# Moving the exp of 3 of 16 key tiles from ScalarE to VectorE in a fused attention and MLP block

## The chip, the cores and the metric

The kernel runs on one core of one Trainium2 chip. The metric is the device time of one execution in microseconds (us). PE is the matmul engine (TensorE) and PEld its weight loads, ACT is ScalarE, DVE is VectorE, POOL is GpSimd. SBUF and PSUM are the memories on the chip that these kernels use; the matmuls write to PSUM. A few executions of each kernel were timed. Executions over 1.5% slower than the fastest of the same kernel are left out of the means. Ratios are the mean time of one kernel's fast runs over the mean of the other's fast runs of the same rounds, on the same chip, so they are not quite the ratios of the medians that are quoted beside them. The rounds ran on several chips; the kernel before stayed within 1122 to 1131 us in all of them, so a difference of two medians from different rounds is good to a few us and no better.

## The reference, cut to what matters

```python
def _A_ref(x, wqkv, wo):                       # B=1, S=2048, D=512, 32 heads of 16
    qkv = (x @ wqkv)...                        # q, k, v: [heads, S, 16]
    scores = jnp.einsum('bhqd,bhkd->bhqk', q, k) * Dh ** (-0.5)
    p = softmax(scores)                        # 32 x 2048 x 2048 exps
    o = jnp.einsum('bhqk,bhkd->bhqd', p, v)
    return o... @ wo
h = layernorm(x) * (1 + ca) + sa               # modulation from silu(c) @ w_mod
x = x + ga * _A_ref(h, A_wqkv, A_wo)
h = layernorm(x) * (1 + cb) + sb
x = x + gb * MLP(h)                            # 512 -> 1376 -> 512, gelu
```

There are 134 million exps against a head dimension of only 16, so the exp is a large share of the work.

## The kernel before

Work goes in 32 *runs*: 4 query blocks of 512, times 8 groups of 4 heads. Each run walks 16 key tiles of 128. For one key tile PE makes the scores of 4 heads as two *QK pairs* (two 32-row matmuls side by side, 128 keys x 512 queries each), ScalarE takes the exp of each pair (one 128x1024 activation), and PE multiplies by V with one *PV unit*: four column-tiled matmuls, one for each head. V has a column of ones, so the softmax denominator comes out of the same matmuls. PE's order is written by hand; the other engines are scheduled by the framework.

```python
stp = tile_pool(name="stp", bufs=3, space=psum)   # score buffers, 128x1024 f32 each
odp = tile_pool(name="odp", bufs=1, space=psum)   # od: PV sum of a run, 128x512 f32
axp = tile_pool(name="axp", bufs=1, space=psum)   # projections and MLP, 128x512 f32
ptp = tile_pool(name="ptp", bufs=3)               # exp tiles (here 4 heads each)
...
def emit_exp(s):
    pt = ptp.tile([P, 4, QB], BF16, name="pt")
    for half in range(2):
        nc.scalar.activation(out=pt[:, 2 * half:2 * half + 2, :], in_=st_of.pop(2 * s + half),
                             func=ACT.Exp, scale=ESC)
...
def emit_pv(s):
    for i in range(4):
        nc.tensor.matmul(out=od[32 * i:32 * i + 32, :], lhsT=VE[kt][:, 8 * cc + 2 * i + par, :],
                         rhs=pt[:, i, :], start=(kt == 0), stop=(kt == NT - 1),
                         tile_position=(0, 32 * i))
...
for s in range(NS):                # one key tile of one run
    emit_exp(s)
    emit_qk(2 * s + 3); emit_qk(2 * s + 4)
    emit_pv(s - 1)
    pop()                          # one piece of a projection, of Wo or of the MLP, if any waits
```

The softmax here doesn't subtract the row's maximum and nothing guards it: scores larger than these inputs give would overflow.

## Time and profile before

| | before |
|---|---|
| time | 1125.75 us (median of 3, 1123.66 to 1128.4) |
| exps on ScalarE | 1024, 0.92 us of busy time each |
| ScalarE idle before exps | 26 us |
| PE clock granted, mean | 0.66 |

The page of the kernel before: the busy line, and the rows of PE, ACT and the granted PE clock over 40 equal slices, each digit in tenths.

```profile
PE 950.4 (85%) x4984; PEld 234.6 (21%) x4984; DVE 193.9 (17%) x364; ACT 985.4 (88%) x1057; POOL 62.9 (6%) x75
...
PE   0678899989999869999999789989898698999856
...
ACT  0367999999999999999999999999999999999801
...
PEclk9988955555557967555558977555558976555568
```

Next the exps as one group of its instructions (busy us, mean ns of one, then the idle time before them and what ended it), and the two waits between PE and the exps (us in total, times, longest).

```profile
L255 ACT ACTIVATE pt<-st 128x1024 bf16<-128x1024 f32 x1024 | 942.1, 1261 | 25.7 <-PE st L248 25.5
```

```profile
PE st L248 <- ACT pt L255: 50.6, 79, 7.8
ACT pt L255 <- PE st L248: 25.5, 28, 1.4
```

ScalarE sets the pace: it is full in every slice between start and tail, and it waits for scores only 28 times. PE is second, and only just: it shows 85% busy. A stretch of its timeline at half clock shows how the time of one key tile (1.83 us, PV at 503.90 to PV at 505.73) is spent.

```profile
503.08 3.89 ACT L255 ACTIVATE pt<-st 128x1024 bf16<-128x1024 f32 x4
503.36 0.61 PE L248 MATMUL st<-qm_3970,kT_0_173 32*128 32x512 bf16 x2
...
503.90 0.62 PE L267 MATMUL od<-pt,VE_190 128*32 128x512 bf16 x4
...
504.45 1.35 PE L248 MATMUL st<-qm_3970,kT_0_173 32*128 32x512 bf16 x4
...
505.73 0.62 PE L267 MATMUL od<-pt,VE_191 128*32 128x512 bf16 x4
```

A QK pair to the next PV takes 0.54 us, a PV to the next pair 0.55 us. So PE needs, by this estimate, about 2 x 0.54 + 0.55 = 1.63 us of the 1.83 us.

### The profile page before, as it was taken

How to read it: one execution, taken by the hardware profiler on the slowest of the kernel's cores; microseconds unless marked ns; L12 is line 12 of the kernel's file. 1: busy time of each engine (PE TensorE's matmuls, PEld its weight loads, DVE VectorE, ACT ScalarE, POOL GpSimd, SP SyncE). 2: the span in 40 equal slices, each digit the busy share in tenths (PEclk: the TensorE clock that was granted, in tenths of full speed). 3: DMA queues.
4: the chain of work that ended last, by engine and by line, in shares of the span. 5: the costliest groups of instructions: out<-in, count | busy, mean ns of one | idle time of the engine just before them, and what ended most of it. 6: DMA issues, size and time to landing. Idle time of an engine off the chain costs nothing.

```text
span 1122.1 us, 12537 instructions
## 1 busy us (share of the span) xinstructions
PE 950.4 (85%) x4984; PEld 234.6 (21%) x4984; DVE 193.9 (17%) x364; ACT 985.4 (88%) x1057; POOL 62.9 (6%) x75
## 2 busy tenths in 40 slices
PE   0678899989999869999999789989898698999856
PEld 0222311111112312111112222111112222111122
DVE  3412200000004411000004311000005211000053
ACT  0367999999999999999999999999999999999801
POOL 5000000000000000000000000000000000000000
PEclk9988955555557967555558977555558976555568
DMA  9300000000000000000000000000000000000000
GB/s 259 104 0 1 11 11 11 11 11 11 11 11 11 11 5 25 11 11 11 11 11 11 12 10 21 11 11 10 11 11 11 11 25 11 6 11 11 11 10 19
DMA packets 27772, 22.25 MB, mean 20 GB/s; under 512 B 13921, under 2 KB 22466, under 8 KB 27714
## 3 DMA queue, kind: packets, MB, share of 16 engines
q1 hardware_dynamic: 24546, 18.83, 5.8%
q10 hardware_dynamic: 3168, 2.62, 0.9%
q8 instruction: 39, 0.64, 0.2%
q14 instruction: 19, 0.16, 0.0%
HBM read 18.81 MB, written 2.62 MB: 19 GB/s over the span
## 4 chain that ended last, share of the span: by engine, by line
ACT 63%; PE 17%; issue 13%; DMA 4%; DVE 2%; SPq 0%; POOL 0%; POOLq 0%; ACTq 0%; DVEq 0%
ACT pt L255 61%; PE st L248 3%; PE ax L199 3%; PE ax L355 3%; PE od L267 2%; PE st L222 2%; DMA xb<-in_A_x_dram 2%; PE st L355 1%; PE st L336 1%; DMA hT<-in_w_mod_dram 1%; DMA W_116<-in_B_w_dram 1%; PE st L404 0%; PE ax L300 0%; ACT big L345 0%; ACT hT L184 0%
## 5 line engine op out<-in xcount | busy, mean ns | idle before, releaser
L255 ACT ACTIVATE pt<-st 128x1024 bf16<-128x1024 f32 x1024 | 942.1, 1261 | 25.7 <-PE st L248 25.5
L276 DVE COPY OD<-od 128x512 f32<-128x512 f32 x32 | 22.2, 692 | 424.2 <-PE od L267 380.3
L289 POOL TENSOR_TENSOR OT<-OD,RB 128x512 bf16<-128x512 f32 x32 | 40.5, 1267 | 912.8 <-DMA RB<-rn 912.8
L345 ACT ACTIVATE big<-big 128x5632 bf16<-128x5632 bf16 x4 | 19.6, 4896 | 37.6 <-DVE big L338 37.6
L355 PE MATMUL ax<-W_116,big 128*128 128x512 bf16 x132 | 39.1, 420 | 0.0
L336 PE MATMUL ax<-big,W_113 128*128 128x512 bf16 x132 | 33.8, 378 | 3.4 <-DVE big L338 2.2
L338 DVE TENSOR_SCALAR big<-ax,b1c 128x512 bf16<-128x512 f32 x33 | 24.8, 751 | 36.7 <-PE ax L336 36.7
L184 ACT ACTIVATE hT<-st,modA 128x512 bf16<-128x512 bf16 x8 | 6.2, 777 | 28.0 <-DVE hT L187 28.0
L199 PE MATMUL ax<-hT,Wq_93 128*128 128x512 bf16 x60 | 24.8, 560 | 0.1
L156 PE MATMUL ax<-sc,hT 128*128 128x1 bf16 x32 | 1.0, 165 | 27.3 <-DVE sc L137 27.3
L222 PE MATMUL st<-Wq_95,hT 128*128 128x512 bf16 x64 | 19.1, 439 | 5.4 <-ACT VE_183 L226 0.7
L359 DVE TENSOR_TENSOR res<-ax,gb_bc 128x512 f32<-128x512 f32 x12 | 8.3, 692 | 87.4 <-PE ax L355 87.4
L336 PEld LDWEIGHTS <-W_113 128*128 128x128 bf16 x176 | 17.0, 99 | 24.5 <-issue 11.7
L281 DVE RECIPROCAL dc<-dc 128x16 f32<-128x16 f32 x32 | 8.0, 251 | 80.7 <-DMA dc<-dn 80.7
L355 PEld LDWEIGHTS <-big 128*128 128x128 bf16 x176 | 15.1, 104 | 30.6 <-issue 15.9
L309 DVE TENSOR_TENSOR res<-ax,ga_bc 128x512 f32<-128x512 f32 x12 | 8.3, 692 | 68.0 <-PE ax L306 68.0
L267 PE MATMUL od<-pt,VE_187 128*32 128x512 bf16 x128 | 18.7, 574 | 0.0
L267 PE MATMUL od<-pt,VE_192 128*32 128x512 bf16 x128 | 18.2, 539 | 0.4 <-ACT pt L255 0.3
L267 PE MATMUL od<-pt,VE_188 128*32 128x512 bf16 x128 | 18.5, 567 | 0.0
L248 PEld LDWEIGHTS <-kT_2_167 32*128 32x128 bf16 x128 | 7.7, 94 | 51.5 <-issue 51.0
L267 PE MATMUL od<-pt,VE_183 128*32 128x512 bf16 x128 | 18.0, 553 | 0.0
L267 PE MATMUL od<-pt,VE_182 128*32 128x512 bf16 x128 | 18.0, 553 | 0.0
(336 smaller groups left out, 1202.3 us busy)
## 6 DMA issues: line engine op xcount, KB each, us to landing
RB<-rn SPq DMA_DIRECT2D x128, 64.0 KB
big<-in_w_mod_dram SPq DMA_DIRECT2D x1, 2048.0 KB
out_dram<-o SPq DMA_DIRECT2D x16, 128.0 KB
xb<-in_A_x_dram ACTq DMA_DIRECT2D x3, 512.0 KB
W_113<-in_B_w_dram SPq DMA_DIRECT2D x1, 1376.0 KB
W_116<-in_B_w_dram SPq DMA_DIRECT2D x1, 1280.0 KB
hT<-in_w_mod_dram ACTq DMA_DIRECT2D x2, 512.0 KB
xb<-in_A_x_dram SPq DMA_DIRECT2D x1, 512.0 KB
```

The source lines that it names most:

```text
L199: nc.tensor.matmul(out=ps, lhsT=w[:, j, cc * P:(cc + 1) * P], rhs=hT[b][:, j, :], start=(j == 0), stop=(j == NC - 1))
L222: nc.tensor.matmul(out=ps, lhsT=hT[b][:, j, tt * P:(tt + 1) * P], rhs=Wq[2][:, j, :], start=(j == 0), stop=(j == NC - 1))
L248: nc.tensor.matmul(out=st[:, g, :], lhsT=kT[cc][kb][rows, ko * P:(ko + 1) * P], rhs=qm[(cc, b, par)][rows, :], start=True, stop=True)
L255: nc.scalar.activation(out=pt[:, 2 * half:2 * half + 2, :], in_=st_of.pop(2 * s + half), func=ACT.Exp, scale=ESC)
L267: nc.tensor.matmul(out=od[32 * i:32 * i + 32, :], lhsT=VE[kt][:, 8 * cc + 2 * i + par, :], rhs=pt[:, i, :], start=(kt == 0), stop=(kt == N ...
L276: nc.vector.tensor_copy(out=OD, in_=od)
L289: nc.gpsimd.tensor_tensor(out=ot, in0=OD, in1=RB, op=ALU.mult)
L309: nc.vector.tensor_tensor(out=y, in0=ps, in1=ga_bc, op=ALU.mult)
L336: nc.tensor.matmul(out=ps, lhsT=W1[:, j, f * P:(f + 1) * P], rhs=state["h"][:, j, :], start=(j == 0), stop=(j == NC - 1))
L338: nc.vector.tensor_scalar(out=state["g"][:, f, :], in0=ps, scalar1=b1c[:, f:f + 1], scalar2=None, op0=ALU.add)
L345: nc.scalar.activation(out=g, in_=g, func=ACT.Gelu_apprx_tanh)
L355: nc.tensor.matmul(out=ps, lhsT=state["g"][:, f, t * P:(t + 1) * P], rhs=W2[:, f, :], start=False, stop=(f == NF - 1))
```

## The change

The intent: VectorE is idle 83% of the time, so let it make some exps. Adding a bias to the scaled score and converting to int16 gives bits that, read as bf16, are a piecewise linear 2^x. To reduce the error (for one reading it lies between -3.9% and +2.0%, for six between -0.12% and +0.07%, worked out from the formula), the integer is shifted by five further amounts, the six bf16 *readings* go through PV with V scaled by six weights, and the sum is the mean. Key tiles 2, 7 and 11 of every run are treated so; the other 13 stay on ScalarE. The diff, cut to its core:

```diff
+    NPH = 6
+    PH_SH = [round(128 * j / NPH) for j in range(NPH)]
+    PH_W = [bf16_round(2.0 ** (-sh / 128)) for sh in PH_SH]
+    DK = [2, 7, 11]
-    stp = tile_pool(name="stp", bufs=3, space=psum)
+    stp = tile_pool(name="stp", bufs=2, space=psum)
+    sdp = tile_pool(name="sdp", bufs=1, space=psum)    # scores for VectorE, 128x1024 f32
-    ptp = tile_pool(name="ptp", bufs=3)                # tiles of 4 heads
+    ptp = tile_pool(name="ptp", bufs=5)                # tiles of 2 heads
+    dpp = tile_pool(name="dpp", bufs=3)                # the readings ph0 to ph5
 ...
+    def emit_dexp(n, r, kt, half):
+        sd = sdp.tile([P, 1024], FP32, name="sd")
+        qk(sd..., r, kt, half)
+        ph0 = dpp.tile([P, 1024], I16, name="ph0")
+        nc.vector.tensor_scalar(out=ph0, in0=sd, scalar1=PH_B, scalar2=0.0,
+                                op0=ALU.add, op1=ALU.max)
+        for j in range(1, NPH):
+            ph = dpp.tile([P, 1024], I16, name=f"ph{j}")
+            nc.vector.tensor_scalar(out=ph, in0=ph0, scalar1=PH_SH[j], scalar2=None, op0=ALU.add)
+        ...                                            # second half: six PV units into pvq
+            for j in range(NPH):
+                pvq.append((r, n + 4, lambda j=j, srcs=srcs: pv(r, kt, j, srcs)))
+    def emit_pv(n, budget):                            # takes ready units, oldest due first
+        ...
+            q = min(ready, key=lambda q: (q[0], q[1]))
 ...
+        for n in range(len(apairs)):                   # one ScalarE exp (2 heads)
+            emit_exp(n)                                # second half: one PV unit into pvq, due n + 1
+            emit_qk(n + 2)
+            for d in dpairs.get(n, ()):
+                emit_dexp(n, *d)
+            emit_pv(n, 3 if len(pvq) > 7 else 2)
+            if r > 0 and n % 3 == 0 or ...: pop()
```

(Cut: the 15 further copies of V, scaled on POOL; loads and tiles rearranged to make room.)

More of the change, by code (lines that the diff above doesn't have):

```diff
@@ L16 @@
 I32 = mybir.dt.int32
+I16 = mybir.dt.int16
 @with_exitstack
@@ L49, with bf16_round, ph_gain @@
     ESC = math.log(2.0) / 128.0
+    NPH = 6
+    PH_SH = [round(128 * j / NPH) for j in range(NPH)]
+    def bf16_round(v):
+        m, e = math.frexp(v)
+        return math.ldexp(round(m * 256) / 256, e)
+    PH_W = [bf16_round(2.0 ** (-sh / 128)) for sh in PH_SH]
+    def ph_gain():
+        tot = 0.0
+        for f in range(128):
+            val = 0.0
+            for sh, w in zip(PH_SH, PH_W):
+                n, m = divmod(f + sh, 128)
+                val += w * 2.0 ** n * (1 + m / 128)
+            tot += val / 2.0 ** (f / 128)
+        return tot / 128
+    PH_B = 127.0 * 128.0 - 128.0 * math.log2(ph_gain())
+    DK = [2, 7, 11]
     psum = bass.MemoryType.PSUM
@@ L53 @@
     keep = ctx.enter_context(tc.tile_pool(name="keep", bufs=1))
-    stp = ctx.enter_context(tc.tile_pool(name="stp", bufs=3, space=psum))
+    stp = ctx.enter_context(tc.tile_pool(name="stp", bufs=2, space=psum))
+    sdp = ctx.enter_context(tc.tile_pool(name="sdp", bufs=1, space=psum))
     odp = ctx.enter_context(tc.tile_pool(name="odp", bufs=1, space=psum))
@@ L59 @@
     work = ctx.enter_context(tc.tile_pool(name="work", bufs=2))
-    ptp = ctx.enter_context(tc.tile_pool(name="ptp", bufs=3))
+    wqp = ctx.enter_context(tc.tile_pool(name="wqp", bufs=3))
+    ptp = ctx.enter_context(tc.tile_pool(name="ptp", bufs=5))
+    dpp = ctx.enter_context(tc.tile_pool(name="dpp", bufs=3))
     x_src = A_x[0].rearrange("(b t p) d -> b p t d", t=TPB, p=P)
@@ L65, with gbuf @@
     nc.scalar.dma_start(out=c_bf, in_=c.rearrange("o (j p) -> p (o j)", p=P))
-    xb = [xin.tile([P, TPB, D], BF16, name="xb", bufs=NQ) for _ in range(NQ)]
+    xb = [xin.tile([P, TPB, D], BF16, name="xb", bufs=2) for _ in range(NQ)]
     nc.sync.dma_start(out=xb[0], in_=x_src[0])
     wm_src = w_mod.rearrange("(j p) n -> p j n", p=P)
-    def big():
-        return work.tile([P, NC * 4 * D], BF16, name="big", bufs=1)
+    def gbuf():
+        return work.tile([P, NF, QB], BF16, name="g", bufs=1)
     def block_tile():
@@ L75 @@
     WmA = [block_tile() for _ in range(2)]
-    WmB = big().rearrange("p (j n) -> p j n", j=NC)
+    wmb = gbuf()
+    WmB = {4: wmb[:, 0:4, :], 3: wmb[:, 4:8, :],
+           2: work.tile([P, NC, D], BF16, name="x2", bufs=1)}
     for i in range(2):
@@ L79 @@
     wq_src = A_wqkv.rearrange("(j p) n -> p j n", p=P)
-    Wq = [keep.tile([P, NC, D], BF16, name=f"Wq{i}") for i in range(3)]
-    for i in (1, 0, 2):
+    Wq = {}
+    for i in (1, 2, 0):
+        Wq[i] = wqp.tile([P, NC, D], BF16, name="Wq")
         nc.sync.dma_start(out=Wq[i], in_=wq_src[:, :, i * D:(i + 1) * D])
@@ L84 @@
         nc.scalar.dma_start(out=xb[b], in_=x_src[b])
-    nc.sync.dma_start(out=WmB, in_=wm_src[:, :, 2 * D:6 * D])
+    for i in (2, 3, 4):
+        nc.sync.dma_start(out=WmB[i], in_=wm_src[:, :, i * D:(i + 1) * D])
     Wo = keep.tile([P, 8, D], BF16, name="Wo")
@@ L96, with load_w2 @@
     nc.sync.dma_start(out=W1[:, :, 0:F], in_=B_w1.rearrange("(j p) n -> p j n", p=P))
-    W2 = keep.tile([P, NF, D], BF16, name="W2")
-    nc.gpsimd.memset(W2[:, NF - 1, :], 0.0)
-    nc.sync.dma_start(out=W2[:, 0:NF - 1, :],
-                      in_=B_w2[0:(NF - 1) * P, :].rearrange("(j p) n -> p j n", p=P))
-    nc.sync.dma_start(out=W2[0:FL, NF - 1, :], in_=B_w2[(NF - 1) * P:F, :])
+    W2 = {}
+    def load_w2():
+        for i in range(3):
+            W2[i] = wqp.tile([P, NC, D], BF16, name="Wq") if i < 2 else keep.tile([P, 3, D], BF16, name="W2c")
+        for i in range(2):
+            nc.sync.dma_start(out=W2[i], in_=B_w2[4 * i * P:4 * (i + 1) * P, :].rearrange("(j p) n -> p j n", p=P))
+        nc.gpsimd.memset(W2[2][:, 2, :], 0.0)
+        nc.sync.dma_start(out=W2[2][:, 0:2, :], in_=B_w2[8 * P:10 * P, :].rearrange("(j p) n -> p j n", p=P))
+        nc.sync.dma_start(out=W2[2][0:FL, 2, :], in_=B_w2[10 * P:F, :])
     b1_bf = const.tile([P, NF], BF16, name="b1_bf")
@@ L175, in ln_rows @@
         nc.gpsimd.tensor_tensor(out=rs, in0=rs, in1=eps_c, op=ALU.pow)
-        z = work.tile([P, TPB, D], BF16, name="ln_z")
+        z = work.tile([P, TPB, D], BF16, name="ln_z", bufs=1)
         for t in range(TPB):
@@ L191 @@
     kT = [[keep.tile([P, QB], BF16, name=f"kT{cc}_{b}") for b in range(NQ)] for cc in range(NC)]
-    VE = [keep.tile([P, 32, 32], BF16, name=f"VE{t}") for t in range(NT)]
+    VW = 17
+    VE = {}
     for t in range(NT):
-        nc.gpsimd.memset(VE[t][:, :, 16:32], 1.0)
+        for ph in (range(NPH) if t in DK else (0,)):
+            v = keep.tile([P, 32 * VW + 15], BF16, name=f"VE{t}_{ph}")
+            nc.gpsimd.memset(v[:, 32 * VW:32 * VW + 15], 0.0)
+            vv = v[:, 0:32 * VW].rearrange("p (h w) -> p h w", w=VW)
+            nc.gpsimd.memset(vv[:, :, 16:17], PH_W[ph] if t in DK else 1.0)
+            VE[(t, ph)] = (v, vv[:, :, 0:16])
     OT = {}
@@ L224, in emit_v @@
         src = ps.rearrange("p (h d) -> p h d", d=16)
-        if eng is nc.scalar:
-            nc.scalar.copy(out=VE[t][:, :, 0:16], in_=src)
-        else:
-            nc.vector.tensor_copy(out=VE[t][:, :, 0:16], in_=src)
-    slots = [(b, u, kt) for b in range(NQ) for u in range(8) for kt in range(NT)]
-    NS = len(slots)
+        if t in DK:
+            vf = work.tile([P, D], FP32, name="vf", bufs=1)
+            nc.vector.tensor_copy(out=vf, in_=ps)
+            vs = vf.rearrange("p (h d) -> p h d", d=16)
+            for ph in range(NPH):
+                nc.gpsimd.tensor_scalar(out=VE[(t, ph)][1], in0=vs, scalar1=PH_W[ph],
+                                        scalar2=0.0, op0=ALU.mult, op1=ALU.add)
+        elif eng is nc.scalar:
+            nc.scalar.copy(out=VE[(t, 0)][1], in_=src)
+        else:
+            nc.vector.tensor_copy(out=VE[(t, 0)][1], in_=src)
+    NA = NT - len(DK)
+    runs = [(b, u) for b in range(NQ) for u in range(8)]
+    apairs = []
+    dpairs = {}
+    for r, (b, u) in enumerate(runs):
+        base = len(apairs)
+        for kt in range(NT):
+            if kt not in DK:
+                apairs += [(r, kt, 0), (r, kt, 1)]
+        for m, kt in enumerate(DK):
+            for half in range(2):
+                at = base + int((2 * m + half + 0.25) * 2 * NA / (2 * len(DK) + 0.5))
+                dpairs.setdefault(at, []).append((r, kt, half))
     st_of = {}
@@ L235, with qk @@
     od_of = {}
-    def emit_qk(n):
-        s, half = divmod(n, 2)
-        if s >= NS:
-            return
-        b, u, kt = slots[s]
+    left = {r: len(DK) * NPH + NA for r in range(len(runs))}
+    begun = set()
+    pvq = []
+    def qk(st, r, kt, half):
+        b, u = runs[r]
         cc, par = divmod(u, 2)
         kb, ko = divmod(kt, TPB)
-        st = st_tile().rearrange("p (g q) -> p g q", g=2)
         for g in range(2):
@@ L249, in emit_qk @@
                              rhs=qm[(cc, b, par)][rows, :], start=True, stop=True)
-        st_of[n] = st
-    def emit_exp(s):
-        pt = ptp.tile([P, 4, QB], BF16, name="pt")
-        for half in range(2):
-            nc.scalar.activation(out=pt[:, 2 * half:2 * half + 2, :], in_=st_of.pop(2 * s + half),
-                                 func=ACT.Exp, scale=ESC)
-        pt_of[s] = pt
-    def emit_pv(s):
-        b, u, kt = slots[s]
-        cc, par = divmod(u, 2)
-        if kt == 0:
-            od_of[(b, u)] = odp.tile([P, QB], FP32, name="od")
-        od = od_of[(b, u)]
-        pt = pt_of.pop(s)
+    def emit_qk(n):
+        if n < len(apairs):
+            st_of[n] = st_tile().rearrange("p (g q) -> p g q", g=2)
+            qk(st_of[n], *apairs[n])
@@ new lines, in emit_exp @@
+    def emit_exp(n):
+        r, kt, half = apairs[n]
+        if half == 0:
+            pt_of[(r, kt)] = []
+        pts = pt_of[(r, kt)]
+        pt = ptp.tile([P, 2, QB], BF16, name="pt")
+        pts.append(pt)
+        nc.scalar.activation(out=pt, in_=st_of.pop(n), func=ACT.Exp, scale=ESC)
+        if half == 1:
+            pvq.append((r, n + 1, lambda: pv(r, kt, 0, [pts[i // 2][:, i % 2, :] for i in range(4)])))
+            del pt_of[(r, kt)]
+    def emit_dexp(n, r, kt, half):
+        sd = sdp.tile([P, 1024], FP32, name="sd")
+        qk(sd.rearrange("p (g q) -> p g q", g=2), r, kt, half)
+        ph0 = dpp.tile([P, 1024], I16, name="ph0")
+        nc.vector.tensor_scalar(out=ph0, in0=sd, scalar1=PH_B, scalar2=0.0,
+                                op0=ALU.add, op1=ALU.max)
+        phs = [ph0]
+        for j in range(1, NPH):
+            ph = dpp.tile([P, 1024], I16, name=f"ph{j}")
+            nc.vector.tensor_scalar(out=ph, in0=ph0, scalar1=PH_SH[j], scalar2=None, op0=ALU.add)
+            phs.append(ph)
+        if half == 0:
+            pt_of[(r, kt)] = phs
+        else:
+            first = pt_of.pop((r, kt))
+            for j in range(NPH):
+                srcs = [t.bitcast(BF16)[:, g * QB:(g + 1) * QB]
+                        for t in (first[j], phs[j]) for g in range(2)]
+                pvq.append((r, n + 4, lambda j=j, srcs=srcs: pv(r, kt, j, srcs)))
@@ L266, in emit_pv, with pv @@
+    def pv(r, kt, ph, srcs):
+        b, u = runs[r]
+        cc, par = divmod(u, 2)
+        if r not in od_of:
+            od_of[r] = odp.tile([P, QB], FP32, name="od")
+        od = od_of[r]
+        start = r not in begun
+        begun.add(r)
+        left[r] -= 1
         for i in range(4):
-            nc.tensor.matmul(out=od[32 * i:32 * i + 32, :], lhsT=VE[kt][:, 8 * cc + 2 * i + par, :],
-                             rhs=pt[:, i, :], start=(kt == 0), stop=(kt == NT - 1),
+            c0 = VW * (8 * cc + 2 * i + par)
+            nc.tensor.matmul(out=od[32 * i:32 * i + 32, :], lhsT=VE[(kt, ph)][0][:, c0:c0 + 32],
+                             rhs=srcs[i], start=start, stop=(left[r] == 0),
@@ L269, in emit_pv @@
                              tile_position=(0, 32 * i))
-        if kt == NT - 1:
-            emit_norm(b, u)
-    def emit_norm(b, u):
-        od = od_of.pop((b, u))
+        if left[r] == 0:
+            emit_norm(r)
+    def emit_pv(n, budget):
+        while pvq and budget > 0:
+            ready = [q for q in pvq if q[1] <= n]
+            if not ready:
+                return
+            q = min(ready, key=lambda q: (q[0], q[1]))
+            if any(p[0] < q[0] for p in pvq):
+                return
+            pvq.remove(q)
+            q[2]()
+            budget -= 1
@@ L275, in emit_norm @@
+    def emit_norm(r):
+        b, u = runs[r]
+        od = od_of.pop(r)
         OD = work.tile([P, QB], FP32, name="OD")
@@ L283, in emit_norm @@
         nc.sync.dma_start(out=rn.rearrange("i (s e) -> (i s) e", e=16), in_=dc)
-        RB = work.tile([P, QB], FP32, name="RB")
+        RB = work.tile([P, QB], FP32, name="RB", bufs=1)
         for i in range(4):
@@ L287, in emit_norm @@
                               in_=rn[i:i + 1, :].to_broadcast([32, QB]))
-        ot = OT[(b, u)] = work.tile([P, QB], BF16, name="OT", bufs=11)
+        ot = OT[(b, u)] = work.tile([P, QB], BF16, name="OT", bufs=9)
         nc.gpsimd.tensor_tensor(out=ot, in0=OD, in1=RB, op=ALU.mult)
     def tail_units(b, alloc, wide):
-        x2 = work.tile([P, TPB, D], BF16, name="x2")
+        x2 = work.tile([P, TPB, D], BF16, name="x2", bufs=1)
         units = []
@@ L307, in wo_b @@
                                  start=False, stop=(u == 7))
-            y = work.tile([P, D], FP32, name="res")
+            y = work.tile([P, D], FP32, name="res", bufs=1)
             nc.vector.tensor_tensor(out=y, in0=ps, in1=ga_bc, op=ALU.mult)
-            nc.vector.tensor_tensor(out=x2[:, t, :], in0=y, in1=xb[b][:, t, :], op=ALU.add)
+            xr = work.tile([P, D], BF16, name="xr")
+            nc.sync.dma_start(out=xr, in_=x_src[b][:, t, :])
+            nc.vector.tensor_tensor(out=x2[:, t, :], in0=y, in1=xr, op=ALU.add)
         for t in range(TPB):
@@ L317, in ln @@
             state["z"] = ln_rows(lambda t: x2[:, t, :], "b")
-            buf = big()
-            state["h"] = buf[:, 0:NC * QB].rearrange("p (j q) -> p j q", j=NC)
-            state["g"] = buf[:, NC * QB:(NC + NF) * QB].rearrange("p (f q) -> p f q", f=NF)
+            state["h"] = block_tile()
+            state["g"] = gbuf()
         units.append((ln, False))
@@ L354, in w2 @@
             for f in range(lo, hi):
-                nc.tensor.matmul(out=ps, lhsT=state["g"][:, f, t * P:(t + 1) * P], rhs=W2[:, f, :],
+                nc.tensor.matmul(out=ps, lhsT=state["g"][:, f, t * P:(t + 1) * P], rhs=W2[f // 4][:, f % 4, :],
                                  start=False, stop=(f == NF - 1))
             if hi == NF:
-                y = work.tile([P, D], FP32, name="res")
+                y = work.tile([P, D], FP32, name="res", bufs=1)
                 nc.vector.tensor_tensor(out=y, in0=ps, in1=gb_bc, op=ALU.mult)
@@ L387, in mods_late, with gate @@
     def mods_late():
-        mod_columns(modB, ((WmB, 1), (WmB, 2)), aux())
+        mod_columns(modB, ((WmB[3], 0), (WmB[4], 0)), aux())
         nc.vector.tensor_scalar(out=modB[:, NC:2 * NC], in0=modB[:, NC:2 * NC], scalar1=1.0,
                                 scalar2=None, op0=ALU.add)
-    def gate(dst, w, h):
+    def gate(dst, i):
+        if i not in WmB:
+            WmB[i] = work.tile([P, NC, D], BF16, name="x2", bufs=1)
+            nc.sync.dma_start(out=WmB[i], in_=wm_src[:, :, i * D:(i + 1) * D])
+            return
+        w, h = WmB[i], 0
         ps = aux()
@@ L429 @@
                 queue.append((f"k{cc}", lambda cc=cc, b=b: emit_k(aux(), cc, b, nc.vector), False))
-        queue.append(("gate", lambda: gate(ga_bc, WmB, 0), False))
+        queue.append(("gate", lambda: gate(ga_bc, 2), False))
         queue.append(("gate", mods_late, False))
-        queue.append(("gate", lambda: gate(gb_bc, WmB, 3), False))
-        for n in range(3):
+        queue.append(("gate", lambda: gate(gb_bc, 5), False))
+        queue.append(("gate", load_w2, False))
+        queue.append(("gate", lambda: gate(gb_bc, 5), False))
+        for n in range(2):
             emit_qk(n)
-        for s in range(NS):
-            b, u, kt = slots[s]
-            cc, par = divmod(u, 2)
-            emit_exp(s)
-            if b == 0 and u == 0 and kt % TPB == 1 and kt < 12:
+        for n in range(len(apairs)):
+            r, kt, half = apairs[n]
+            b, u = runs[r]
+            at = n % (2 * NA)
+            emit_exp(n)
+            if r == 0 and half == 0 and kt % TPB == 0 and kt < 12:
                 nb = kt // TPB + 1
@@ L443 @@
                     zs[nb + 1] = ln_rows(lambda t: xb[nb + 1][:, t, :], "a")
-            if s + 2 < NS:
-                nb2, nu2, _ = slots[s + 2]
-                need(f"k{nu2 // 2}")
-                need(f"q{nu2 // 2}_{nb2}")
-            emit_qk(2 * s + 3)
-            emit_qk(2 * s + 4)
-            if s > 0:
-                emit_pv(s - 1)
-            if b == 0 and u == 0:
-                if kt >= 12:
-                    pop()
-            else:
+            if n + 4 < len(apairs):
+                b2, u2 = runs[apairs[n + 4][0]]
+                need(f"k{u2 // 2}")
+                need(f"q{u2 // 2}_{b2}")
+            emit_qk(n + 2)
+            for d in dpairs.get(n, ()):
+                emit_dexp(n, *d)
+            emit_pv(n, 3 if len(pvq) > 7 else 2)
+            if r > 0 and n % 3 == 0 or r == 0 and at > 2 * NA - 6:
                 pop()
-            if u == 0 and kt == 10 and b > 0:
+            if b > 0 and u == 0 and at == 18:
                 for fn, cont in tail_units(b - 1, aux, False):
                     queue.append(("tail", fn, cont))
-            if u % 2 == 1 and kt == 6:
+            if u % 2 == 1 and at == 4:
                 nc2, nb2 = (u // 2 + 1, b) if u < 7 else (0, b + 1)
@@ L463 @@
                     push_front(f"q{nc2}_{nb2}", lambda cc=nc2, b=nb2: emit_q(aux(), cc, b))
-        emit_pv(NS - 1)
+        while pvq:
+            emit_pv(1 << 30, 1)
         while queue:
```

## The prediction

> **What bounds the kernel now.** ScalarE. In the page's busy line ACT is at 985 us of 1122 (88%), PE 950 (85%), VectorE 194 (17%). The largest group is the exp of the scores: 1024 activations of 128x1024, 942 us, 0.92 us each; they have only 26 us of idle before them, and they hold 61% of the chain of waits. They begin 48 us into the span (timeline) and end about 64 us before its end (slices). PE looks busy, but in pure attention stretches (250 to 290, 500 to 530 us) its granted clock is 0.50 and it keeps up even so.
>
> **What the change moves.**
> - ScalarE: 832 exps instead of 1024. 192 x 0.92 = 177 us leave it.
> - VectorE: 192 units, each one 128x1024 reading of PSUM and five 16-bit additions in SBUF. From the trace, a VectorE instruction costs about 0.16 us plus 0.53 us per 512 f32 elements of PSUM (copy 692 ns), about 0.06 us more per pointer scalar[...].[...] Estimate: 1.23 + 5 x 0.43 = 3.35 us a unit, 643 us in all, VectorE about 840 us busy. In a tail stretch (Wo, MLP) it then needs 1.14 times ScalarE's time per run of 16 key tiles; elsewhere about 0.91.
> - PE: PV units (four column-tiled matmuls) per run go from 16 to 31; 4096 matmuls of attention become 6016 (QK unchanged). At full clock, with 0.11 us for each switch between QK and PV shapes (a PV unit to the next QK takes 0.32 us warm, 0.55 cold), a run needs about 18 us plus 4 us of projections and MLP; at clock 0.5 about 31 us plus 8. ScalarE needs 23.9 us.
> - PSUM: score buffers for ScalarE fall from 3 to 2, so a projection burst (4 full matmuls, near 0.95 us) between two QK pairs shows as a ScalarE stall, about 0.4 us for each of some 175.
>
> **How much is on the path.** All 177 us are, but three engines end up within some 15% of each other and wait for one another in order. Sum: 48 start + 765 exps + 70 projection stalls + 40 VectorE-bound tails + 50 block inputs and gelus + 25 low-clock stretches + 64 tail = 1062; I take 1055.
>
> **The clock decides much.** [...]the records here hold only 0.5 and 1.0. In this trace, windows of attention alone fall back to 0.5 and rise when 128x128 matmuls come in.[...]
>
> **Time:** 1055 us, range 970 to 1150; faster by over 2%: 0.70; within 2%: 0.17; slower: 0.13.
>
> **What would show it right:** 832 exps at 0.92 us, ACT busy near 808 us with 100 to 150 us more idle before exps, mostly behind PE; the 16-bit additions near 0.43 us, the PSUM reading near 1.23 us; VectorE over 75% busy; mean granted clock up from 0.66 to about 0.85; PV matmuls 3968.
>
> **What would make it wrong:** the 16-bit additions at half that rate (VectorE 1050 us or more, then slower than before); the clock staying at 0.5 in attention (PE-bound, about 1150 us); waits of PE for the single projection buffer or the single VectorE score buffer; or, the other way, stalls hidden well, near 980.

Two of its figures stand as estimates: the mean clock of 0.85, and the 0.43 us for an addition. The second can be estimated from the trace of the kernel before. There a copy of 512 f32 elements out of PSUM took 692 ns, the same with a pointer scalar 751 ns, an aggregate over 6 elements 168 ns; the 0.16, 0.53 and 0.06 us agree with these. ln_z (512 bf16 elements, two pointer scalars) took 407 ns: less 0.16 and 2 x 0.06 us, that leaves 0.13 us, so 1024 elements without a pointer would take about 0.16 + 0.26 = 0.42 us.

The times for PE are estimates as well, and the traces come near them. At full clock the trace of the changed kernel has 0.23 us from one PV unit to the next and 0.32 us from a PV unit to a QK pair (medians), so about 0.1 us more where the shape changes; at half clock 0.40 us, and 0.15 us more. 63 units a run at 0.22 us with 35 changes of shape come to about 17 us at full clock, at 0.40 us to about 30 us. The 128x512 matmuls of projections and MLP start 0.216 us apart at full clock and 0.43 us at half clock (medians in the kernel before, which has 680 of them: 4.6 and 9 us a run). A QK pair follows the last of a burst after 0.31 us at full clock: 3 x 0.216 + 0.31 = 0.96 us. The stall of 0.4 us for each burst is a mere estimate; dk0, with two score buffers, has 85 waits of exps for scores, 82 us in all. As to the clock, in the exp loop of the kernel before 177 of 193 periods of its records without a 128x128 matmul were at 0.5, and 67 of 103 with one at 1.0.

## The result, and the profile after

| | before | after |
|---|---|---|
| time (median) | 1127.08 us | 1277.05 us (1271.78 to 1289.86) |
| ratio | | 1.135 (95%: 1.125 to 1.145) |
| exps on ScalarE, idle before them | 1024, 26 us | 832, 325 us |
| VectorE busy | 194 us | 761 us |
| PE clock granted, mean | 0.66 | 0.75 |

The change made the kernel 13.5% slower. The page of the changed kernel: the busy line and the same rows.

```profile
PE 990.6 (78%) x6843; PEld 248.0 (20%) x6904; DVE 761.4 (60%) x1517; ACT 839.6 (66%) x864; POOL 74.4 (6%) x139
...
PE   2668888888888876887787886887888886878856
...
ACT  1456766777777768877766677667777767777711
...
PEclk9888766656659688887768687687659778697578
```

The busy line has 6843 records of 6904 matmuls. No engine is full any longer: between start and tail ScalarE is at 6 to 8 tenths in every slice, PE at 6 to 8. That is the picture of engines that wait for each other in turn. The exps' group and the largest waits among PE, ScalarE and VectorE in the loop:

```profile
L328 ACT ACTIVATE pt<-st 128x1024 bf16<-128x1024 f32 x832 | 796.9, 1027 | 325.2 <-PE od L364 184.2 <-PE st L313 128.5 <-PE sd L313 10.0
```

```profile
ACT pt L328 <- PE od L364: 184.2, 95, 3.7
PE st L313 <- ACT pt L328: 129.8, 201, 7.6
ACT pt L328 <- PE st L313: 128.5, 141, 4.5
PE od L364 <- DVE OD L386: 64.6, 31, 2.9
```

The first wait did not exist before. An exp does not *read* od; it waits for a PV matmul because that matmul reads the exp tile (pt) it wants to write into. With five tiles in turn (each holds 2 heads, so two and a half key tiles), the exp stands still until an older tile has been through PV. The timeline shows why that takes long (cut to matmuls and exps):

```profile
299.20 0.60 PE L313 MATMUL st<-qm_2648,kT_2_183 32*128 32x512 bf16 x2
...
299.74 0.61 PE L364 MATMUL od<-ph_2937,VE_4_203 128*32 128x512 bf16 x2
299.74 0.61 PE L364 MATMUL od<-ph_3009,VE_4_203 128*32 128x512 bf16 x2
...
300.13 0.64 PE L364 MATMUL od<-ph_2939,VE_5_206 128*32 128x512 bf16 x2
300.14 0.64 PE L364 MATMUL od<-ph_3011,VE_5_206 128*32 128x512 bf16 x2
...
301.25 0.62 PE L364 MATMUL od<-pt,VE_0_215 128*32 128x512 bf16 x4
...
301.65 0.44 PE L364 MATMUL od<-pt,VE_0_218 128*32 128x512 bf16 x4
301.96 1.94 ACT L328 ACTIVATE pt<-st 128x1024 bf16<-128x1024 f32 x2 [2.54 <-PE od L364]
...
303.04 0.39 PE L313 MATMUL st<-qm_2648,kT_2_183 32*128 32x512 bf16 x2 [0.95 <-ACT pt L328]
```

The PV units of VectorE's readings (inputs named ph) are due first and go first; the PV units of the exp tiles (input named pt) come after them. ScalarE has been idle for 2.54 us when the first of these (301.25) has been through and a tile is free. Then PE is idle for 0.95 us, because it has no score buffer until that exp is done.

VectorE itself did what was forecast. One unit, from the timeline:

```profile
303.68 1.23 DVE L337 TENSOR_SCALAR ph_3111<-sd 128x1024 int16<-128x1024 f32 x1 [3.79 <-PE sd L313]
304.94 0.43 DVE L342 TENSOR_SCALAR ph_3113<-ph_3111 128x1024 int16<-128x1024 int16 x1
305.28 0.42 DVE L342 TENSOR_SCALAR ph_3115<-ph_3111 128x1024 int16<-128x1024 int16 x1
```

The reading of the scores in PSUM takes 1.23 us and an addition 0.42 us (the medians of 192 and of 960 are the same; 13 additions took 0.6 to 1.5 us). The additions start 0.34 us apart, so a unit costs about 1.23 + 5 x 0.34 = 2.9 us, a little under the forecast 3.35 us. VectorE waited 3.79 us for its scores here: it does not set the pace at this place.

### The profile page after: what moved, and what is told of

The parts are those of the page before. It is cut to its first block, busy times and chain, and to the rows that moved or that the text cites. A ratio compares the mean times of both kernels' runs of the same rounds, so it can differ in the third digit from the quotient of the medians.

```text
span 1270.0 us, 17728 instructions
## 1 busy us (share of the span) xinstructions
PE 990.6 (78%) x6843; PEld 248.0 (20%) x6904; DVE 761.4 (60%) x1517; ACT 839.6 (66%) x864; POOL 74.4 (6%) x139
## 4 chain that ended last, share of the span: by engine, by line
PE 54%; ACT 20%; DVE 14%; issue 9%; DMA 2%; POOL 0%; ACTq 0%; SPq 0%; POOLq 0%; DVEq 0%
PE od L364 22%; PE st L313 18%; ACT pt L328 17%; PE ax L466 2%; PE ax L447 2%; PE ax L247 2%; DVE OD L386 2%; ACT g L456 2%; PE st L270 1%; DMA xb<-in_A_x_dram 1%; PE ax L416 1%; PE st L466 1%; PE ax L410 1%; PE st L447 1%; PE sd L313 1%
## 5 line engine op out<-in xcount | busy, mean ns | idle before, releaser
L328 ACT ACTIVATE pt<-st 128x1024 bf16<-128x1024 f32 x832 | 796.9, 1027 | 325.2 <-PE od L364 184.2
L456 ACT ACTIVATE g<-g 128x5632 bf16<-128x5632 bf16 x4 | 19.6, 4896 | 37.1 <-DVE g L449 37.0
L447 PE MATMUL ax<-hT,W_125 128*128 128x512 bf16 x116 | 39.7, 453 | 3.3 <-issue 1.3
L449 DVE TENSOR_SCALAR g<-ax,b1c 128x512 bf16<-128x512 f32 x33 | 24.6, 746 | 26.6 <-PE ax L447 26.6
L247 PE MATMUL ax<-hT,Wq 128*128 128x512 bf16 x99 | 33.5, 462 | 3.5 <-issue 2.0
L466 PE MATMUL ax<-Wq,g 128*128 128x512 bf16 x85 | 26.4, 427 | 1.8 <-issue 1.6
L270 PE MATMUL st<-Wq,hT 128*128 128x512 bf16 x62 | 18.7, 431 | 7.7 <-DVE vf L275 1.2
L466 PEld LDWEIGHTS <-g 128*128 128x128 bf16 x176 | 15.1, 105 | 33.8 <-issue 19.1
L247 PEld LDWEIGHTS <-Wq 128*128 128x128 bf16 x128 | 11.9, 110 | 34.7 <-issue 27.7
L212 DVE BATCH_NORM_STATS2 ln_s<-xb 128x6 f32<-128x512 bf16 x16 | 10.3, 681 | 13.2 <-DMA xb<-in_A_x_dram 13.2
```

The source lines that it names most:

```text
L247: nc.tensor.matmul(out=ps, lhsT=w[:, j, cc * P:(cc + 1) * P], rhs=hT[b][:, j, :], start=(j == 0), stop=(j == NC - 1))
L270: nc.tensor.matmul(out=ps, lhsT=hT[b][:, j, tt * P:(tt + 1) * P], rhs=Wq[2][:, j, :], start=(j == 0), stop=(j == NC - 1))
L328: nc.scalar.activation(out=pt, in_=st_of.pop(n), func=ACT.Exp, scale=ESC)
L447: nc.tensor.matmul(out=ps, lhsT=W1[:, j, f * P:(f + 1) * P], rhs=state["h"][:, j, :], start=(j == 0), stop=(j == NC - 1))
L449: nc.vector.tensor_scalar(out=state["g"][:, f, :], in0=ps, scalar1=b1c[:, f:f + 1], scalar2=None, op0=ALU.add)
L456: nc.scalar.activation(out=g, in_=g, func=ACT.Gelu_apprx_tanh)
```

## The experiments

Three theories were to be told apart. **PE theory:** the 15 extra PV units of each run (31 instead of 16) are on the path. **Buffer theory:** ScalarE starves because buffers were cut (score buffers from 3 to 2) or are held too long (five exp tiles behind the PV order). **VectorE theory:** VectorE's queue is late with the od copy and with its score buffer. All 14 kernels gave results within the tolerance of the comparison with the reference. "Before" is the kernel before in the same rounds, with medians of 1124 to 1129 us.

### 1. dk0: the rearranged code without any VectorE exp

```diff
-    DK = [2, 7, 11]
+    DK = []
```

> The restructured code with no key tile on VectorE (all 1024 exps on ScalarE, two score buffers instead of three, half-size exp tiles). If the restructuring is harmless: 1125 us, within 2% of the kernel before. If the third score buffer mattered (each projection burst then stalls ScalarE by about 0.4 us): 1170 to 1200 us, ScalarE idle before exps up from 26 to 100 us.

Measured: 1214.23 us, ratio 1.078 (1.075 to 1.082). The waits of ScalarE on PE:

```profile
ACT pt L328 <- PE st L313: 82.3, 85, 2.3
```

The rearrangement alone loses about 90 us, with all exps still on ScalarE: the second reading of the expectation, though 14 us above its range. The exps wait 82 us for scores instead of 26, and none of them waits for od, so exp tiles are not scarce here. Start to start, exps are 921 ns apart at the median instead of 905 (read off the trace); over 1024 exps that would be another 16 us.

### 2. pv1_add5: VectorE's work kept, its extra PV units dropped

```diff
+    NPV = 1
-    left = {r: len(DK) * NPH + NA for r in range(len(runs))}
+    left = {r: len(DK) * NPV + NA for r in range(len(runs))}
-            for j in range(NPH):
+            for j in range(NPV):        # PV units for the first reading only
```

(The bias is matched to one reading, so the result is a valid, coarser one.)

> VectorE does all it did (reading and five additions, the additions unused), but only one of the six readings goes into PV: PV units per run fall from 31 to 16. If PE's extra PV work (its time and its place in PE's order) is the cause: 1050 us or less, ScalarE idle before exps under 170 us. If VectorE's load is the cause (late od copy, late score buffer): it stays above 1200 us.

Measured: 1053.38 us (3 us above the range of the first reading), ratio 0.937 (0.934 to 0.939). VectorE is as busy as in the changed kernel (764 us), yet the kernel is faster than before. The VectorE theory is out as the main cause; what hurts comes in with the extra PV units.

### 3. pv6_add0: the additions dropped, the extra PV units kept

```diff
-        for j in range(1, NPH):
-            ph = dpp.tile(...); nc.vector.tensor_scalar(out=ph, in0=ph0, ...)
-                        for t in (first[j], phs[j]) for g in range(2)]
+                        for t in (first[0], phs[0]) for g in range(2)]
```

(The bias is matched to the one reading here too.)

> VectorE makes one reading only (no additions, about 1.2 us a unit instead of 3.0), but PV still has 31 units a run, all six on the same reading. PE theory: 1200 to 1280 us, little gained but the wait of PV for the od copy (65 us of PE idle in the changed kernel) shrinks to under 30. VectorE theory: 1100 us or less.

Measured: 1242.36 us, ratio 1.104 (1.101 to 1.107). The additions are worth only 35 us. PE's wait for the od copy falls from 65 to 28 us, about as much as those 35:

```profile
PE od L360 <- DVE OD L382: 28.1, 31, 1.7
```

### 4. pt_first: another order of the same PV units

```diff
-            q = min(ready, key=lambda q: (q[0], q[1]))
+            q = min(ready, key=lambda q: (q[0], q[3], q[1]))   # q[3]: 0 for ScalarE's, 1 for VectorE's
```

> Only the order of PV units on PE changes: a ready unit of ScalarE's exps goes before ready units of VectorE's. If ScalarE starves because its five exp tiles stay occupied behind six VectorE-fed PV units: the 184 us of waiting for od fall below 60 and the time below 1200 us. If PE's capacity at half clock is the bound: within 2% of 1277 us, the wait turns up elsewhere.

Measured: 1188.49 us, ratio 1.057 (1.052 to 1.062). PE does exactly the same work and 89 us are gone; the wait of exps for od disappears from the list. A part of it returns as waiting for scores (219 us instead of 128):

```profile
L328 ACT ACTIVATE pt<-st 128x1024 bf16<-128x1024 f32 x832 | 797.3, 1034 | 238.7 <-PE st L313 218.9 <-PE sd L313 17.0 <-ACT pt L328 0.3
```

So the extra units hurt first by *where they stand* in PE's order.

### 5. pv3_add5: three readings in PV

As pv1_add5, with `NPV = 3`.

> As the run with one reading in PV (1053 us), but three of the six readings go into PV: 22 PV units a run instead of 16 (31 in the changed kernel). If every PV unit is paid on the path, at 0.47 us each (224 us over 480 units, from the first runs): 1053 + 192 x 0.47 = 1143 us. If PE has slack up to some point and only the last units hurt: under 1090 us.

Measured: 1089.75 us, ratio 0.967 (0.964 to 0.970). The first 192 added units cost 36 us (0.19 us each), the next 288, up to the changed kernel, 187 us (0.65 us each). The cost is not linear. With three readings no exp waited for od, with six they waited 184 us: somewhere between, a batch of VectorE's units grows long enough to hold back the exp tiles.

### 6. pv6_add0_pt12: twelve exp tiles

pv6_add0 with `ptp` at 12 tiles instead of 5 (there is room, as five readings are not made).

> As the run with one reading used six times (1242 us), but with 12 exp tiles instead of 5 (there is room without the other readings). If ScalarE stops because its exp tiles are not released in time: the 193 us of waiting for od fall under 30 and the time by 80 to 110 us, as much as reordering gave. If the wait only showed that PE was behind: it moves to the score buffers and the time stays within 2% of 1242 us.

Measured: 1122.38 us, ratio 0.994 (0.989 to 0.999). 120 us less than with five tiles (more than the 80 to 110 expected), with unchanged order and unchanged PE work; the wait for od is gone. No other single repair gained as much. The exps' group, with five tiles and with twelve:

```profile
L328 ACT ACTIVATE pt<-st 128x1024 bf16<-128x1024 f32 x832 | 795.6, 1028 | 297.4 <-PE od L360 193.3 <-PE st L313 94.1 <-PE sd L313 6.6
L328 ACT ACTIVATE pt<-st 128x1024 bf16<-128x1024 f32 x832 | 797.8, 1034 | 179.6 <-PE st L313 163.1 <-PE sd L313 14.0 <-ACT pt L328 0.3
```

The mean granted clock rose with it, from 0.75 to 0.80, as it did in the runs of pt_first and pt7 (0.78 and 0.77, the changed kernel 0.75). How much of such a gain comes by way of the clock was not separated.

### 7. pt_first_od_act: the od copy on ScalarE

```diff
-        nc.vector.tensor_copy(out=OD, in_=od)
+        nc.scalar.copy(out=OD, in_=od)
```

> On top of the reordered PV units (1188 us): the copy of od out of PSUM goes to ScalarE, not behind VectorE's queue. PE's 65 us of waiting for that copy fall under 35. If that wait is on the path: 1145 to 1170 us (ScalarE pays 32 x 0.6 = 19 us for it). If not: 1190 us or more.

Measured: 1138.78 us, ratio 1.013 (1.008 to 1.017), 50 us less than pt_first and less than the 1145 to 1170 expected. Once per run PE cannot start the next PV sum before the single od buffer is copied out, and that copy stood in VectorE's queue behind a unit of about 3 us. The wait fell only from 65 to 40 us:

```profile
PE od L364 <- ACT OD L386: 39.5, 31, 1.6
```

So the gain is larger than the wait that was removed. The exps' wait for scores fell too, from 219 to 160 us, and the granted clock rose from 0.78 to 0.81; what links these was not settled.

### 8. nph1_sh3: one reading, three shared score buffers

```diff
-    NPH = 6
+    NPH = 1
-    stp ... bufs=2 ; sdp ... bufs=1 ; ptp ... bufs=5
+    stp ... bufs=3 ;                  ptp ... bufs=9
-        sd = sdp.tile([P, 1024], FP32, name="sd")
+        sd = st_tile()                 # QK pairs of both engines take the three buffers in turn
```

(The loop is changed so that the QK pairs of both engines are issued in one fixed order.)

> A version that uses the findings: one reading per key (no additions, no extra PV), and three score buffers shared by ScalarE and VectorE in turn, nine exp tiles. From 1053 us for one reading with two buffers: less VectorE queueing (a few us) and the third buffer (dk0 paid about 70 us of projection stalls) gives 960 to 1010 us. If VectorE holds the shared buffer too long: 1040 us or more.

Measured: 1005.07 us, ratio 0.893 (0.889 to 0.897), within the range expected and 48 us less than pv1_add5. The additions, the score buffers and the exp tiles all changed here, so the run does not say which of them gave the 48 us.

### 9. dk0_sh3: dk0 with three score buffers

dk0 with the buffers of experiment 8 (three score buffers, nine exp tiles).

> The restructured code with no VectorE exp (1214 us with two score buffers and five exp tiles), but three score buffers and nine exp tiles. If the third score buffer is what the restructuring lost: within 2% of the kernel before, 1125 to 1145 us (16 us stay for ScalarE's extra wait per exp, 921 ns start to start instead of 905). If another part of the restructuring costs (order of projections, half-size exp tiles): 1190 us or more.

Measured: 1119.21 us, ratio 0.994 (0.991 to 0.997), 6 us below the range expected: the 16 us that were to stay did not (the exps are 903 ns apart at the median again, read off the trace). The exps' wait for scores is back to the value before:

```profile
ACT pt L327 <- PE st L312: 25.5, 32, 1.5
```

So all that the rearrangement lost was buffers, 95 us. The run changed score buffers and exp tiles together; since no exp of dk0 waited for an exp tile, the score buffer is the likely one, but the two were not run apart.

### 10. pt7: the changed kernel with seven exp tiles

```diff
-    ptp = tile_pool(name="ptp", bufs=5)
+    ptp = tile_pool(name="ptp", bufs=7)      # room from three scratch tiles
```

> The changed kernel with seven exp tiles instead of five, nothing else in its order (room from three small scratch tiles). Exp-tile theory: ScalarE's 184 us of waiting for od fall to under 100 us, the time to 1180 to 1225 us. PE-capacity theory: within 2% of 1277 us.

Measured: 1179.86 us, ratio 1.049 (1.043 to 1.055). 97 us for two more tiles of 2 KB a partition, in the same order. The exps' group (idle 325 us in the changed kernel):

```profile
L328 ACT ACTIVATE pt<-st 128x1024 bf16<-128x1024 f32 x832 | 797.7, 1034 | 245.2 <-PE st L313 227.1 <-PE sd L313 15.9
```

This is just below the range of the exp-tile theory (1180 to 1225 us). The 184 us of waiting for od are gone to nothing; 99 us of them turned into waiting for scores.

### 11. pt7_first_od_act: tiles, order and copy together

Experiments 4, 7 and 10 in one kernel.

> All three repairs on the changed kernel with its six readings: seven exp tiles, ScalarE's PV units first, od copied by ScalarE. The reordering and the tiles repair the same wait, so little is added to 1139 us: 1110 to 1140 us, not faster than the kernel before by more than 2%, because the two score buffers (about 88 us) and the PV units (about 70 us) stay.

Measured: 1141.56 us, ratio 1.014 (1.008 to 1.020), 1.6 us above the range expected and no better than order and copy alone (1138.78 us). Tiles and order repair the same wait.

### 12. nph1_sh3_dk5: five key tiles on VectorE

nph1_sh3 with `DK = [2, 5, 7, 10, 13]`.

> One reading, three shared score buffers, five key tiles on VectorE instead of three (704 exps on ScalarE). If ScalarE still sets the pace (1005 us at three tiles, 0.92 us an exp): 128 x 0.92 = 118 us less at most, 900 to 940 us. If PE at half clock sets it[...]: 970 to 1010 us.

(The cut held the author's estimate of PE's time for a run, with a figure for a PV unit that no trace shows. At half clock the trace of the changed kernel has 0.40 us from a PV unit to the next and 0.57 us to a QK pair, that of the kernel before 0.55 us to a QK pair; medians.)

Measured: 965.47 us, ratio 0.859 (0.855 to 0.863), the fastest version found. The further gain over three tiles is 40 us, not 118: ScalarE is at 75% busy, and its exps wait 134 us for scores. PE is what most of their waiting is for, as the second reading of the expectation said (the time is just under its range).

### 13. six_sh3: the changed kernel with three shared score buffers only

> The changed kernel with three score buffers shared by ScalarE and VectorE in turn (instead of two for ScalarE and one for VectorE in the same space), five exp tiles and the old order kept. If the third score buffer is worth as much as without VectorE exps (95 us): about 1185 us. If ScalarE's starving for exp tiles hides it: 1240 us or more.

Measured: 1298.84 us, ratio 1.151 (1.146 to 1.155). A miss for the first reading: the third score buffer, which with more exp tiles was worth 95 us without VectorE exps, brings nothing here; the run is 22 us slower than the changed kernel.

```profile
ACT pt L327 <- PE od L363: 226.9, 94, 5.5
ACT pt L327 <- PE st L312: 136.6, 122, 7.9
```

The wait for exp tiles has grown (184 us before) and the time with it. Whether a repair shows can depend on a tighter ring in front of it: the next run makes the same edit once that ring is repaired.

### 14. six_sh3_all: six readings with all repairs

Three shared score buffers, seven exp tiles, ScalarE's PV units first, od copied by ScalarE.

> Six readings with all repairs: three shared score buffers, seven exp tiles, ScalarE's PV units first, od copied by ScalarE. If the pieces add (1142 us less the 95 us of the score buffer): 1045 to 1075 us, faster than the kernel before. If PE's 31 PV units a run bound it: 1110 us or more.

Measured: 1106.41 us, ratio 0.981 (0.976 to 0.987). The result lies between the two readings, nearer to the second. With everything repaired, six readings stand 1.9% below the kernel before. Against pt7_first_od_act, which differs by the shared score buffers alone, it is 35 us less (1141.56 to 1106.41): the edit that cost 22 us in six_sh3 gains here. That is still well under the 95 us of dk0_sh3. The exps still wait 157 us for scores:

```profile
L327 ACT ACTIVATE pt<-st 128x1024 bf16<-128x1024 f32 x832 | 787.6, 1047 | 158.1 <-PE st L312 156.7 <-ACT pt L327 0.3
```

## Why the prediction was wrong

It forecast 1055 us in 970 to 1150, with 0.13 for slower; measured were 1277 us.

**What was right.** The costs of the instructions: 832 exps, 1.23 us for the reading of PSUM, 0.42 us for an addition (forecast 0.43), 3968 PV matmuls, ACT busy near 808 us (840, as the exps took 0.96 us of busy time each and not 0.92). So an addition over 1024 16-bit elements in SBUF took about a third of the reading of 1024 f32 elements in PSUM, as estimated. The term "70 projection stalls" stood for the lost score buffer; dk0 against dk0_sh3 measured 95 us for the buffers (without VectorE exps).

**The step that failed** is "How much is on the path". Its sum set 177 us of freed ScalarE time against three terms, and it took PE's doubled PV work as hidden, since "a run needs about 18 us plus 4 us" at full clock against ScalarE's 23.9 us. That compares totals. It has no term for the order of PE's queue and the number of tiles that it holds. A VectorE key tile puts six PV units in front of ScalarE's own, ScalarE owns five exp tiles, and so it stops while PE works through them; PE then stops for want of a score buffer. Forecast were "100 to 150 us more idle before exps"; measured were 299 more (26 to 325 us), 184 of them for exp tiles. In place of a hidden cost the runs show:

- Exp tiles held behind VectorE's PV units: 97 us (two more tiles), 89 us (other order) or 120 us (twelve tiles, in the kernel without additions). The list of "what would make it wrong" named the projection buffer and VectorE's score buffer, but not this ring. (PE's waits in the changed kernel list none for VectorE's score buffer.)
- The od copy behind VectorE's queue: 65 us of PE waiting and 50 us of time. Also without a term.
- The PV units themselves: with the buffers repaired, six readings stand at 1106 us and one reading at 1005 us. 101 us over 480 units is about 0.21 us each. This is a rough estimate, as the additions, the tile counts, the order and the engine of the od copy also differ between the two; the first 192 units of pv3_add5, with no exp waiting for od, cost about as much (0.19 us each).
- "40 VectorE-bound tails" did not show: VectorE was 60% busy, not the forecast "over 75%", and taking all additions away gained 35 us, which the shorter wait for the od copy covers.

**The clock** was named as what "decides much". Forecast was a mean of "about 0.85", an estimate for which no trace gave a ground, and measured was 0.75; 125 of 175 periods with attention alone were at half clock. What this cost the changed kernel stays open. For those 175 (the 3.41 us periods of the clock records, inside the exp loop, without a 128x128 matmul) exps can be counted: counted by their starts there is an exp in each 1.39 us at half clock and in each 1.33 us at full clock, but counted by their ends it is 1.33 and 1.48 us. So this count does not show that the faster clock helped or that it did not. In six_sh3_all both ways agree: 1.25 to 1.28 us (70 periods) and 1.04 us (68), faster at full clock. Of the four executions of the changed kernel those with the lower clock took longer (1271.78 us at 0.751, 1289.86 us at 0.727). No run could hold the clock fixed, so cause and effect are not separated.

**Where the expected gain went.** Most of the freed ScalarE time did arrive. From dk0 (1214 us) to pv1_add5 (1053 us) the move of 192 exps brought 161 us of the 177, with all of VectorE's work in place. The rearrangement had taken about 90 us before, and the PV units of the five further readings gave back 224 us (1053 to 1277), about half of it for want of exp tiles (97 to 120 us). The repairs in a row give the same picture: 1277 us, 1142 with tiles, order and od copy, 1106 with the shared score buffers as well. What is left open: how far one reading is accurate enough. The comparison with the reference accepts it, but attention enters the output through a small gate, so that says little about another model.

## What to carry to other kernels

When work is moved to an idle engine, don't only add up each engine's busy time: for every ring of buffers, ask what now stands in the consumer's queue before the instruction that releases it, and give the ring as many tiles as the longest such batch needs. Weigh what the move takes from the bound engine's rings to make room; here the buffers taken cost 95 us (dk0 against dk0_sh3), where moving the exps brought 161. And when one repair shows nothing, look for a tighter ring in front of it before calling it useless: the shared score buffers lost 22 us before the other repairs and gained 35 after them.

## What else the traces show

- In the kernel before, from 250 to 290 us, PE was 37.0 of 40 us busy by the records and the granted clock stayed at 0.50. So busy time in the records alone did not raise it. In that trace 177 of the 193 clock periods in the exp loop without a 128x128 matmul were at half clock; in six_sh3_all, with more PV units, only 70 of 138 were. What raises the clock was not settled.
- In the changed kernel, at half clock, one PV unit follows another in 0.39 us (299.74 to 300.13) but a PV unit follows a QK pair in 0.54 us (299.20 to 299.74): about 0.15 us more where the shape changes (medians of that trace at half clock: 0.40 and 0.54 us).
- In the changed kernel VectorE's additions of 0.42 us started 0.34 us apart (medians).
- In the changed kernel 514 exps started before the one in front had ended, and overlapped it by 112 ns at the median (an exp of 1017 ns, for example, and the next one 904 ns after its start).
